# Top-32 attention with a token MLP on one core: the last batch in groups of three, three and two tiles instead of a group of its own for the last rows

## The chip, the cores and the metric

The kernel runs on one core of one Trainium2 chip. The metric is the device time of one execution in microseconds (us), the median of several runs.

## The reference

Eight batches, eight heads, 576 rows, head size 64, all float32. Each row of scores keeps its 32 largest values, a softmax is taken over these, and the values are weighed with it. The heads are put side by side into rows of 512, and a channel MLP with a normalization and a residual follows.

```python
scores = scale * np.matmul(q, k.transpose(0, 1, 3, 2))       # (8, 8, 576, 576)
kth = np.partition(scores, -32, axis=-1)[..., -32:-31]
scores = np.where(scores >= kth, scores, -1000000000.0)
scores = scores - np.max(scores, axis=-1, keepdims=True)
attn = np.exp(scores)
attn = attn / (np.sum(attn, axis=-1, keepdims=True) + 1e-09)
x = np.matmul(attn, v)                                       # then (8, 576, 512)
mu, var = mean and variance of x over the last axis          # cut
xn = (x - mu) / np.sqrt(var + 1e-06) * g_ln
out = x + np.maximum(xn @ w_ch1, 0.0) @ w_ch2                # 512 -> 2048 -> 512
```

## The kernel before

576 rows are four tiles of 128 rows (0 to 3) and one of 64, the "last rows" (tile `J = 4`). The kernel takes two heads at a time, so a batch has four head pairs (`hp`). A **unit** is one query tile of one head pair: its scores (TensorE), the choice of 32 values (VectorE, eight at a time), the mask and the exponential (ScalarE), and the turning of the weights so that keys lie on partitions. A unit of last rows holds both heads in one tile, and so is half of an ordinary one for VectorE. A **group** is the units of one job of one head pair that share one product with the values. The program is a loop over the units with index n, one step to each; the scores of a unit are made two steps ahead, and what follows its selection one to four steps behind.

The jobs are listed so:

```python
    for b in range(B):
        parts = [[0, 1], [2, 3], [J]]
        if b:
            parts = [[0, 1], [2, 3]]
            if b == B - 1:
                parts = [[J]] + parts
            else:
                parts[b < 2].append(J)
        for qts in parts:
            jobs += [Job(b, hp, [qts]) for hp in range(NHP)]
```

So batches 2 to 6 run the groups 0, 1, J for the four head pairs and then 2, 3 for the four; batch 7 runs J alone for four head pairs, then 0, 1, then 2, 3. There are 160 units, 20 to a batch.

From batch 2 on all units of a group but its last are turned by VectorE and DMA, not by TensorE (`moved`); a unit of last rows is never moved:

```python
    for u in units[jobs[5 * NHP].first :]:
        u.moved = not u.rest and u is not u.group.units[-1]
    ...
    def move(u):                       # moved: two VectorE transposes, then DMA out and back
        for t in range(2):
            nc.vector.transpose(blocks..., u.e[:, t, t * R : t * R + JP]...)
        nc.sync.dma_start(hbm[:], blocks)
        ...
    def turn(u):                       # not moved: four TensorE transposes to each head
        ...
                nc.tensor.transpose(ps[...], u.e[...], ident[:])
```

The product with the values is 9 matmuls whose width is the number of rows of the group, `g.nq`: 256, 320 or 64.

```python
    def values(g):
        for c in range(J):
            for h in range(2):
                nc.tensor.matmul(av[h * D : (h + 1) * D, 0 : g.nq], vb[:, h * J + c, :], ...)
        nc.tensor.matmul(av[:, 0 : g.nq], g.job.ends[:], g.pt[:, 2 * J, 0 : g.nq], ...)
```

When the last head pair of a group is through, its finished rows become a **block** of one, two or three tiles for the MLP. The last rows of two batches, 64 and 64, make one tile ("r"), which joins the block of the odd batch's group with J in it. The block's matmuls go into a list, `todo`, and are laid between the steps of the attention as filling work:

```python
    # block of n tiles, N = n * 128 rows; 4 chunks of 512 features, NF = 16 chunks of 2048
    hidden:  NF * NC = 64 matmuls, each N columns wide        # planned cost max(1.71e-3 * N, 0.31)
    project: n * NF matmuls, each 512 columns wide            # planned cost 1.71e-3 * 512
    turn:    n times 4 transposes                             # planned cost 0.44
    ...
            step = j.last + (3 if j.last < EARLY else 4)      # the step at which the block is given
            if J in j.groups[0].qts and b % 2:
                step += 1
                tiles.append(("r", b // 2))
    ...
    def slot(n):                       # filling work for each of the 8 slots of step n
        left = sum(t[1] for t in todo)
        if n > last_give:
            even = left / max(1, END - 1 - n)
        else:
            even = 99.0
            for m in sorted(gives):
                if m > n:
                    even = min(even, (left - RESERVE) / (m - n))     # RESERVE = 4.0
                    left += sum(b.cost() for b in gives[m])
        return max(0.0, even) / SLOTS
```

`slot` takes the smallest of the mean rates up to each later block, so that the filling work never runs out before a new block comes. The last block, tiles 2 and 3 of batch 7, is given at step 163; almost all of it runs after the attention is over. The list is worked off in order.

Of the kernel before, what the change touches and what calls it, by code (L numbers as in the profile page):

```python
# [21 lines left out]
J = 4  # L22
# [7 lines left out]
def kernel(  # L30
# [43 lines left out]
    B, H, S, D = q.shape  # L74
# [406 lines left out]
    def turn(u):  # L481

        g = u.group
        i0 = place_of(u)
        q0 = i0 * 32

        def part(t):
            ps = turned()
            for c in range(J):
                nc.tensor.transpose(  # L490
                    ps[:, c * P : (c + 1) * P], u.e[:, t, c * P + t * R : (c + 1) * P + t * R],
                    ident[:],
                )
            if u.rest:
                both = ps[:].rearrange("p (c h n) -> p h c n", h=2, n=R)
                for h in range(2):
                    nc.scalar.copy(
                        g.blocks[:, h, i0 : i0 + R // 32],
                        both[:, h].rearrange("p c (i n) -> p i c n", n=32),
                    )  # L500
            else:
                nc.scalar.copy(
                    g.blocks[:, t, i0 : i0 + P // 32],
                    ps[:].rearrange("p (c i n) -> p i c n", c=J, n=32),
                )

        def last():
            ps = turned()
            if u.rest:
                nc.tensor.transpose(ps[0:R, 0:P], u.e[:, 0, JP:S], ident[:])  # L510
                nc.tensor.transpose(ps[:, P : 2 * P], u.e[:, 0, JP - R : S], ident[:])
                for h in range(2):
                    nc.scalar.copy(  # L513
                        g.pt[h * R : (h + 1) * R, 2 * J, q0 : q0 + R],
                        ps[h * R : (h + 1) * R, h * (P + R) : h * (P + R) + R],
                    )
            else:
                ends = u.e[:].rearrange("p t n -> p (t n)")[:, JP : JP + P]
                nc.tensor.transpose(ps[:, 0:P], ends, ident[:])
                nc.scalar.copy(g.pt[:, 2 * J, q0 : q0 + P], ps[:, 0:P])  # L520

        heads = () if u.moved else range(len(u.tiles))
        return [lambda t=t: part(t) for t in heads] + [last]
# [206 lines left out]
    for b in range(B):  # L730
        parts = [[0, 1], [2, 3], [J]]
        if b:
            parts = [[0, 1], [2, 3]]
            if b == B - 1:
                parts = [[J]] + parts
            else:
                parts[b < 2].append(J)
        for qts in parts:
            jobs += [Job(b, hp, [qts]) for hp in range(NHP)]
    units = []  # L740
# [36 lines left out]
    for j in jobs:  # L777
        if j.hp == NHP - 1:
            b = j.b
# [114 lines left out]
    for n in range(END):  # L894
# [9 lines left out]
        parts = turn(ex) if ex else []  # L904
# [142 lines left out]
```

## Time and profile before

| | before |
|---|---|
| median of 3 runs | 1666.45 us |
| lowest, highest | 1665.65, 1667.94 us |
| span of the profiled execution | 1666.6 us |
| instructions profiled | 24932 |
| mean granted TensorE clock | 0.978 |

A float32 matmul of this kernel shows as two MATMUL records (a transpose as one). The ends of matmul records are modelled, so the time from the start of one record to the start of the next says more than its length. The first MAX8 of line L391 of a unit on VectorE is taken as the start of that unit's step, and all steps below are counted by it: unit 76 is the first of the last four units of batch 3, units 120 to 139 are batch 6, units 140 to 159 are batch 7.

### The profile page before, as it was taken

To read this page: it belongs to the slowest core of one execution; us is meant where nothing else is said; L and a number is where in the kernel's file an instruction comes from. 1 tells how busy PE (TensorE), PEld (TensorE's weight loads), DVE (VectorE), ACT (ScalarE), POOL (GpSimd) and SP (SyncE) were. 2 spreads that over 40 slices of the span, in tenths; PEclk is the share of its full clock that TensorE was granted. 3 is DMA by queue.
4 is the path that set the end of the run, shared out by engine and by line. 5 is a ranking of instruction groups with operands and counts; after the bars stand their busy time and mean duration, and the time that the engine had idled before them with its cause. 6 is when DMAs were issued, how large, how long until landed. Compare 5 with 4: busy or idle time off the path is not lost.

```text
span 1666.6 us, 24932 instructions
## 1 busy us (share of the span) xinstructions
PE 1566.9 (94%) x7057; PEld 941.7 (57%) x7057; DVE 1469.6 (88%) x4611; ACT 1042.4 (63%) x2615; POOL 671.5 (40%) x881
## 2 busy tenths in 40 slices
PE   2668989989899999999999999999999999999998
PEld 1336457556355474745547575745547575756764
DVE  5997999999999999999999999999879895988600
ACT  6886877667556665666656665656555565666620
POOL 5776763343442433343243433443243423333110
PEclk9879999999999999999999999999999999999999
DMA  7423332001442335333443335324333251222200
GB/s 176 106 72 95 85 64 58 21 14 22 100 110 84 99 85 132 93 88 89 108 123 92 86 104 126 97 71 99 99 97 97 72 115 46 61 78 70 80 13 13
DMA packets 303185, 139.30 MB, mean 84 GB/s; under 512 B 250820, under 2 KB 285640, under 8 KB 303048
## 3 DMA queue, kind: packets, MB, share of 16 engines
q1 hardware_dynamic: 298312, 137.12, 31.2%
q10 hardware_dynamic: 4736, 0.59, 0.3%
q8 instruction: 57, 0.93, 0.2%
q14 instruction: 80, 0.66, 0.1%
HBM read 92.54 MB, written 45.09 MB: 83 GB/s over the span
## 4 chain that ended last, share of the span: by engine, by line
PE 65%; DVE 23%; ACT 4%; issue 4%; POOL 3%; DMA 1%; SPq 0%; ACTq 0%; POOLq 0%; DVEq 0%
PE hps L664 23%; PE ops L680 22%; PE scps L354 7%; DVE m L399 7%; PE av L544 6%; DVE hi L386 6%; DVE hi L391 3%; DVE lo L386 2%; PE tp L490 2%; PE av L551 2%; DVE hi L375 2%; DVE size L193 1%; ACT sc L335 1%; POOL lo L376 1%; ACT e L426 1%
## 5 line engine op out<-in xcount | busy, mean ns | idle before, releaser
L664 PE MATMUL hps<-xT,w 128*128 128x256 f32 (+2 forms) x2176 | 553.3, 398 | 6.0 <-ACT xT L653 6.0
L680 PE MATMUL ops<-w,h 128*128 128x512 f32 x1152 | 548.0, 603 | 0.0
L399 DVE MAX8 m<-hi 128x8 f32<-128x304 f32 x1152 | 487.6, 458 | 3.3
L664 PEld LDWEIGHTS hps<-xT,w 128*128 128x128 f32 x2176 | 388.8, 192 | 111.4 <-issue 32.3
L376 POOL TENSOR_TENSOR lo<-sc,hi 128x576 int32<-128x576 int32 (+1 forms) x160 | 207.8, 1299 | 486.3 <-DVE hi L375 246.5
L386 DVE MATCH_REPLACE8 hi<-m,hi 128x304 f32<-128x304 f32 x864 | 389.4, 456 | 0.0
L680 PEld LDWEIGHTS ops<-w,h 128*128 128x128 f32 x1152 | 201.2, 192 | 187.2 <-issue 182.7
L391 DVE MAX8 hi<-lo 128x8 f32<-128x288 f32 x576 | 233.7, 441 | 39.3 <-POOL lo L379 38.2
L354 PE MATMUL scps<-kT,qT 64*128 64x288 f32 (+3 forms) x1344 | 220.7, 429 | 37.1 <-DVE qT L306 27.4
L335 ACT COPY sc<-scps 128x288 f32<-128x288 f32 x576 | 199.7, 408 | 68.2 <-PE scps L354 55.9
L426 ACT ACTIVATE e<-sc,m 128x576 f32<-128x576 f32 x288 | 224.1, 779 | 7.2 <-DVE m L399 4.0
L436 ACT ACTIVATE e<-e,bias 128x576 f32<-128x576 f32 x288 | 224.8, 781 | 0.7
L379 POOL TENSOR_TENSOR lo<-lo,sc 128x576 int32<-128x576 int32 (+1 forms) x160 | 206.9, 1293 | 12.5
L354 PEld LDWEIGHTS scps<-kT,qT 64*128 64x128 f32 (+1 forms) x1344 | 122.3, 179 | 152.9 <-issue 57.6
L544 PE MATMUL av<-pt,vb 128*64 128x256 f32 (+2 forms) x1152 | 148.8, 401 | 0.2 <-ACT pt L513 0.2
L675 ACT ACTIVATE h<-hps 128x512 f32<-128x512 f32 (+1 forms) x156 | 88.5, 567 | 86.1 <-PE hps L664 84.8
L375 DVE TENSOR_TENSOR hi<-sc 128x576 f32<-128x576 f32 (+1 forms) x160 | 115.0, 719 | 23.4 <-ACT sc L335 23.4
L556 ACT COPY oT<-av 128x256 f32<-128x256 f32 (+2 forms) x72 | 26.8, 372 | 160.3 <-PE av L551 160.3
L693 POOL TENSOR_TENSOR o<-o,x 128x512 f32<-128x512 f32 x32 | 42.0, 1313 | 209.6 <-ACT o L689 209.6
L386 DVE MATCH_REPLACE8 lo<-hi,lo 128x288 f32<-128x288 f32 x288 | 125.2, 441 | 0.0
L490 PE MATMUL tp<-ident,e 128*128 128x128 f32 x608 | 97.0, 284 | 25.3 <-ACT e L436 24.8
L544 PEld LDWEIGHTS av<-pt,vb 128*64 128x64 f32 x1152 | 76.0, 142 | 78.5 <-ACT sc L335 14.5
(70 smaller groups left out, 1259.5 us busy)
## 6 DMA issues: line engine op xcount, KB each, us to landing
turned<-sc SPq DMA_DIRECT2D x68, 512.0 KB, 2.6
pt<-turned SPq DMA_DIRECT2D x272, 128.0 KB, 3.0
vb<-in_v_dram SPq DMA_DIRECT2D x144, 128.0 KB, 2.6
raw<-in_moe_w_ch_dram SPq DMA_DIRECT2D x32, 512.0 KB, 4.0
kin<-in_k_dram SPq DMA_DIRECT2D x128, 72.0 KB, 2.5
qin<-in_q_dram SPq DMA_DIRECT2D x120, 72.0 KB, 2.5
out_dram<-o SPq DMA_DIRECT2D x32, 256.0 KB, 2.2
ends<-in_v_dram SPq DMA_DIRECT2D x144, 16.0 KB, 2.2
```

Of the source, the lines that this page charges most:

```text
L335: nc.scalar.copy(u.sc[:, t, s * HALF : (s + 1) * HALF], made[s][t][:, 0:HALF])
L354: nc.tensor.matmul(ps[i * R : i * R + ql, o : o + width], qT[r, q0 : q0 + ql], kT[r, k0 : k0 + width], start=True, stop=True,)
L376: nc.gpsimd.tensor_tensor(lo.bitcast(I32), a.bitcast(I32), hi.bitcast(I32), ALU.subtract)
L379: nc.gpsimd.tensor_tensor(lo.bitcast(I32), lo.bitcast(I32), b.bitcast(I32), ALU.add)
L386: nc.vector.match_replace(x[:, t], m[:, t, :], x[:, t], LOWEST)
L391: nc.vector.max(u.hi[:, t, o : o + 8], u.lo[:, t])
L399: nc.vector.max(m[:, t, :], u.hi[:, t])
L426: nc.scalar.activation(u.e[:, t], u.sc[:, t], AF.Prelu, bias=u.thr[:, t, 7:8], scale=-1.0, alpha=SLOPE)
L436: nc.scalar.activation(u.e[:, t], u.e[:, t], AF.Exp, bias=u.bias[:, t : t + 1], scale=-scale / SLOPE, accum_out=g.den[:, col : col + 1],)
L544: nc.tensor.matmul(av[h * D : (h + 1) * D, 0 : g.nq], vb[:, h * J + c, :], g.blocks[:, h, 0 : g.nq // 32, c, :], start=(c == 0), stop=False,)
L664: nc.tensor.matmul(ps["h"][:, o : o + N], w1[:, c, f * P : (f + 1) * P], xT[0][:, c, 0:N], start=(c == 0), stop=(c == NC - 1),)
L680: nc.tensor.matmul(ps[i][:], hT[f][:, i * P : (i + 1) * P], w2[:, f, :], start=(f == 0), stop=(f == NF - 1),)
```

## The change

Batch 7 loses its exception and is cut as batches 2 to 6 are: groups 0, 1, J for four head pairs, then 2, 3. The number of units stays 160, that of groups falls by four, and that of blocks by one: the tile of the last rows of batches 6 and 7 no longer is a block of its own early in batch 7, but the third tile of the block of tiles 0 and 1. The aim is that no group and no block has fewer than two tiles, so that no matmul of the MLP or of the values is narrower than 256 columns in these batches.

```diff
@@ -731,10 +731,7 @@
         parts = [[0, 1], [2, 3], [J]]
         if b:
             parts = [[0, 1], [2, 3]]
-            if b == B - 1:
-                parts = [[J]] + parts
-            else:
-                parts[b < 2].append(J)
+            parts[b < 2].append(J)
         for qts in parts:
             jobs += [Job(b, hp, [qts]) for hp in range(NHP)]
     units = []
```

## The prediction

> **What bounds the kernel now.** I read the page first, then the busy times by stage, then TensorE's own waits, then the pitch of single matmuls in the timeline.
>
> ```profile
> PE 1566.9 (94%) x7057; PEld 941.7 (57%) x7057; DVE 1469.6 (88%) x4611; ACT 1042.4 (63%) x2615; POOL 671.5 (40%) x881
> ...
> PE   2668989989899999999999999999999999999998
> ...
> DVE  5997999999999999999999999999879895988600
> ```
>
> TensorE is busy to the end; VectorE is nearly as busy up to about slice 29 and has holes after it. A busy TensorE need not be a full one, so I set two stages side by side: units 76 to 115 (from four units before batch 4 to the sixteenth of batch 5) and units 116 to 155 (the same places one double batch later), then the rest. Busy times of each engine in these three stretches:
>
> ```profile
> core 0: us, PE busy (x) PEld busy (x) DVE busy (x) ACT busy (x) POOL busy (x), PEclk, DMA share, GB/s
> 742.10:1114.20 372.10, 369.47 (x1631) 216.48 (x1630) 366.76 (x1152) 236.62 (x608) 145.09 (x203) 1.00 0.37 100
> 1114.20:1525.00 410.80, 407.47 (x1913) 246.87 (x1912) 363.13 (x1145) 245.40 (x629) 145.33 (x208) 1.00 0.31 83
> 1525.00:1666.60 141.60, 135.66 (x545) 87.59 (x543) 40.01 (x130) 46.48 (x107) 20.18 (x29) 0.99 0.12 36
> ```
>
> The first stretch has VectorE at 98.6% and TensorE at 99.3%, the second, 38.7 us longer, has VectorE at 88% and TensorE at 99%. So VectorE may be a second bound up to unit 115, but not after it. TensorE's own waits from unit 116 to the end (total us, times, longest):
>
> ```profile
> PE tp L648 <- ACT sc L335: 2.3, 3, 1.0
> PE hps L664 <- ACT xT L653: 1.1, 1, 1.1
> PE tp L490 <- ACT e L436: 0.4, 1, 0.4
> ```
>
> TensorE waits for some 4 us in the last 552. Is it full too? From the pitches below I gave every record the time its columns take (0.107 us a transpose, 0.215 us for 256 columns, half of that where two heads share the array) and summed: 343.0 us of work in the first stretch, 378.1 in the second, 131.5 in the third. Divided by the wall that is 0.922, 0.920 and 0.929. The three agree, and what is missing is spread over changes from one kind of matmul to another, not over waits. So **TensorE's work is the bound over all of the last 924 us**, and a change is worth what it takes from that work.
>
> The pitches, from the timeline of TensorE:
>
> ```profile
> 1018.77 2.37 PE L544 MATMUL av<-pt,vb 128*64 128x320 f32 x16
> 1021.07 0.81 PE L551 MATMUL av<-pt,ends 128*128 128x320 f32 x2
> 1021.72 1.02 PE L680 MATMUL ops<-w,h 128*128 128x512 f32 x2
> ...
> 1370.12 1.95 PE L544 MATMUL av<-pt,vb 128*64 128x256 f32 x16
> 1371.99 0.70 PE L551 MATMUL av<-pt,ends 128*128 128x256 f32 x2
> 1372.53 1.02 PE L680 MATMUL ops<-w,h 128*128 128x512 f32 x2
> ...
> 1400.94 0.69 PE L544 MATMUL av<-pt,vb 128*64 128x64 f32 x16
> 1401.55 0.43 PE L551 MATMUL av<-pt,ends 128*128 128x64 f32 x2
> 1401.82 0.60 PE L490 MATMUL tp<-ident,e 128*128 128x128 f32 x4
> 1402.27 0.27 PE L510 MATMUL tp<-ident,e 128*64 128x128 f32 x1
> ```
>
> From the start of a values product to the start of what follows it: 2.95 us at 320 columns, 2.41 at 256, 0.88 at 64. Four transposes take 0.45 us, 0.11 each. For the MLP's hidden layer (128 records to a block):
>
> ```profile
> 1498.61 2.17 PE L664 MATMUL hps<-xT,w 128*128 128x128 f32 x18
> 1500.62 0.27 PE L519 MATMUL tp<-ident,e 128*128 128x128 f32 x1
> ...
> 1605.94 27.89 PE L664 MATMUL hps<-xT,w 128*128 128x256 f32 x128
> 1633.67 27.63 PE L680 MATMUL ops<-w,h 128*128 128x512 f32 x64
> ```
>
> 18 records of the one-tile block in 2.01 us, 0.112 each; 128 of the two-tile block in 27.73 us, 0.217 each; 64 records of the projection in about 27.5, 0.43 each. The median pitch at 384 columns is 0.323.
>
> **What the Trainium skill says.** "Perfetto Trace Analysis", section Identifying the Most-Contended Engine, warns that matmul busy time does not tell how near TensorE is to its limit. The trace agrees: the 256-wide hidden records have a mean length of 385 ns at a pitch of 217, hence the sum of columns above. The same page, section Optimizing Tensor Performance, Matmuls, says that larger matmuls are more efficient where possible. That is the reason for the change; but "TensorE: Matmul & The Clock Gate", section Back-to-back issue gap, has the spacing grow with the columns, with a floor only at small widths (about 60 cycles up to 64 columns). Here 128 columns cost 0.112 us and 256 cost 0.217, a ratio of 1.94, so the one-tile block wasted little. Only the 64-wide values product shows a floor: a fifth of the columns at 0.30 of the time of 320.
>
> **The change part by part.**
>
> Values: four times 0.88 + 2.41 becomes four times 2.95. Saved 4 x 0.34 = 1.4 us of TensorE.
>
> Hidden layer: 128 x 0.112 + 128 x 0.217 = 42.1 us becomes 128 x 0.323 = 41.3. Saved 0.7 us. Projections and turns of the rows are the same in number.
>
> Turning: tile 1 of batch 7 is no longer the last of its group, so four more units are moved. Each drops 8 transposes: 32 x 0.11 = 3.5 us of TensorE, and the changes of kind around eight runs of transposes, which I put at 8 x 0.15 = 1.2 us (an estimate from the missing 8% of the stretches above). ScalarE loses 8 copies of 0.58 us, off the path.
>
> VectorE gains two transposes to each of the four units. The mean of one is 685 ns (89.3 us over 136 of them, line L468): 8 x 0.685 = 5.5 us. The DMA out and back is what batches 2 to 6 have, with TensorE not waiting for it. Loads of values fall from twelve sets to eight in batch 7, off the path.
>
> Where the work lies: the larger thing that moves. By the planned costs a block of one tile is 34.3 us, of two 56.9, of three 85.4. Before, at step 116, the smallest mean rate is the one up to step 163: (85.4 + 3 x 56.9 + 34.3 + 56.9) / 47 = 7.4 us a step. After, nothing new comes between steps 143 and 156, so the smallest is the one up to 156: (85.4 + 3 x 56.9) / 40 = 6.4 us, the rate that units 76 to 115 have now. Up to step 156 the program therefore repeats that stretch, and the three-tile block is left for seven steps at 85.4 / 7 = 12.2 us each. Up to step 116 nothing should change.
>
> That gives a second way to the time. Unit 156 starts at 1114.2 + 372.1 = 1486.3 us instead of 1525.0, 38.7 us earlier; the first stretch has five projection records fewer than the new one will have, 2.1 us, so 1488.4. What filling work is then left: before, 13 projection records and two blocks of two, 5.6 + 2 x 55.9 = 117.4 us. After, 16 records left over as at step 116 (6.9), the block of three (41.3 + 41.3 + 1.3 = 83.9) and the block of two (55.9), 146.7 us. The difference of 29.3 us, at 0.945 (the third stretch without the last 4 us, in which TensorE has ended), is 31 us. The end: 1488.4 + 141.6 + 31 = 1661.
>
> The first way: 1.4 + 0.7 + 3.5 + 1.2 = 6.8 us of work less, 1666.45 - 6.8 = 1659.6. The two agree within 1.5 us. **I predict 1660 us**, 0.4% faster.
>
> **The rivals.**
>
> VectorE becomes the bound (it has 5.5 us more, and 98.6% in the stretch that is repeated): its added time then lies on the path up to unit 155 and the work pushed to the end is not made up for: 1666 to 1670. For it speaks VectorE's share in the first stretch; against it, that TensorE's share of columns is 0.92 there too, so little TensorE time was lost.
>
> The crowded end: with 12.2 us of filling in a step of which VectorE needs 9 to 10, scores come late, units 156 to 159 take about 15 us each, and the last block starts late. If TensorE waits in the chain values, statistics, centring, of the last tiles, some 5 us are lost: 1665. Against it: six projections are kept for that chain, and 18 records (7.7 us) cover it today.
>
> Batch 7 was poor before: it takes 203.6 us from unit 140 to the end of its selection, batch 5 takes 186.7, and units 142 and 144 of the trace need 14.4 and 17.5 us. If those were lost time and not filling work, some 17 us come back: 1649. Against it: batch 6, cut as the others, takes 208.9 us at the same higher rate of filling, and TensorE has no wait above 1.1 us there.
>
> **Range and chances.** The savings are some 7 us if TensorE stays full; losing the chain at the end or to VectorE costs up to 6, and a better mesh gives up to 5. The range is 1655 to 1666. A change of 2% is 33 us, far outside any of these: 0.01 faster, 0.98 within, 0.01 slower.
>
> **What would show it.** Right: the same times up to unit 116; batch 6 at about 186 us instead of 208.9; unit 156 near 1488; then 15 us a unit with VectorE waiting; 576 transposes on L490 instead of 608, and 144 on L468 instead of 136; no 128-wide hidden records, and 64-wide values products in batch 0 alone; TensorE busy at 94% or a little more. Wrong: unit 156 later than 1493 (VectorE is the bound), TensorE waits of several us after unit 156, or work per column other than 0.92 of the wall.

## The result and the profile after

| | before | after |
|---|---|---|
| median | 1666.05 us (1664.49 to 1667.94, 4 runs) | 1659.92 us (1658.31 to 1660.92, 4 runs) |
| ratio, 95% interval | | 0.9962 (0.9945 to 0.9979) |
| span of the profiled execution | 1666.6 us | 1655.8 us |
| instructions profiled | 24932 | 24475 |

The change brings 6.1 us, 0.4%. First the page of the changed kernel, busy times and slices:

```profile
PE 1559.2 (94%) x6825; PEld 918.0 (55%) x6825; DVE 1472.6 (89%) x4619; ACT 1036.8 (63%) x2607; POOL 673.9 (41%) x879
...
PE   2668989989899999999999999999999999999998
...
DVE  5997999999999999999999999999999999997000
```

TensorE is as full as it was. VectorE no longer has holes: it is at 9 up to slice 36 and then stops, where before it had 5 to 8 in seven of the ten slices from 29 to 38. The same three stretches as in the prediction (units 76 to 115, 116 to 155, the rest), and batch 6 as a fourth; the columns are those of the table shown there:

```profile
739.70:1111.40 371.70, 369.63 (x1632) 216.59 (x1631) 366.34 (x1151) 236.51 (x609) 145.33 (x203) 1.00 0.37 100
1111.40:1484.70 373.30, 371.57 (x1641) 217.37 (x1640) 367.28 (x1151) 237.31 (x611) 144.93 (x203) 1.00 0.36 99
1484.70:1655.80 171.10, 165.47 (x584) 94.64 (x582) 40.96 (x132) 50.07 (x116) 22.41 (x32) 1.00 0.10 32
1150.50:1337.90 187.40, 186.77 (x802) 104.90 (x801) 183.04 (x574) 117.52 (x301) 72.47 (x102) 1.00 0.37 100
```

The second stretch now is a copy of the first, in time (373.3 and 371.7 us), in number of matmuls and in VectorE's work; before it took 410.8. The rest takes 171.1 instead of 141.6. What was gained by unit 155 was mostly paid after it, and the difference is the result: from unit 116 to the end 552.4 us became 544.4. The profiled execution was already 2.4 us ahead of that of before at unit 76, where nothing has changed; so from here on the stretch from unit 116 to the end stands beside the medians.

TensorE's waits from unit 116 to the end (total us, times, longest):

```profile
PE hps L664 <- ACT xT L653: 1.3, 2, 1.1
PE xo L583 <- ACT oT L556: 0.9, 2, 0.5
```

2.2 us instead of 4.1: the waits of L648, the turn of a block's rows, are gone. The groups that changed (count, then busy us and mean ns):

```profile
L664 PE MATMUL hps<-xT,w 128*128 128x256 f32 x1536 | 370.3, 386 | 3.0 <-ACT xT L653 3.0
...
L664 PE MATMUL hps<-xT,w 128*128 128x384 f32 x512 | 180.8, 493 | 3.2 <-ACT xT L653 3.2
...
L468 DVE STREAM_TRANSPOSE sc<-e 128x512 f32<-128x512 f32 x144 | 95.0, 697 | 21.4 <-ACT e L436 21.1
L490 PE MATMUL tp<-ident,e 128*128 128x128 f32 x576 | 92.0, 284 | 24.7 <-ACT e L436 24.2 <-ACT sc L335 0.5
...
L544 PE MATMUL av<-pt,vb 128*64 128x320 f32 x448 | 66.5, 439 | 0.0
...
L544 PE MATMUL av<-pt,vb 128*64 128x64 f32 x64 | 2.7, 228 | 0.2 <-ACT pt L513 0.2
```

There are 576 transposes on L490 and 144 on L468, no hidden record of 128 columns, and the 64-wide values products of batch 0 alone.

### The profile page after: what moved, and what is told of

It reads as the page before. It is cut to its first block, busy times and chain, and to the rows that moved or that the text cites. A ratio compares the mean times of both kernels' runs of the same rounds, so it can differ in the third digit from the quotient of the medians.

```text
span 1655.8 us, 24475 instructions
## 1 busy us (share of the span) xinstructions
PE 1559.2 (94%) x6825; PEld 918.0 (55%) x6825; DVE 1472.6 (89%) x4619; ACT 1036.8 (63%) x2607; POOL 673.9 (41%) x879
## 4 chain that ended last, share of the span: by engine, by line
PE 71%; DVE 18%; issue 4%; ACT 4%; POOL 3%; DMA 1%; ACTq 0%; POOLq 0%; DVEq 0%
PE hps L664 25%; PE ops L680 24%; PE scps L354 8%; PE av L544 7%; DVE m L399 5%; DVE hi L386 4%; DVE hi L391 3%; PE tp L490 2%; PE av L551 2%; DVE lo L386 2%; DVE hi L375 1%; DVE size L193 1%; PE tp L648 1%; ACT sc L335 1%; PE xo L583 1%
## 5 line engine op out<-in xcount | busy, mean ns | idle before, releaser
L664 PE MATMUL hps<-xT,w 128*128 128x256 f32 (+1 forms) x2048 | 551.1, 412 | 6.1 <-ACT xT L653 6.1
L680 PE MATMUL ops<-w,h 128*128 128x512 f32 x1152 | 548.7, 603 | 0.0
L399 DVE MAX8 m<-hi 128x8 f32<-128x304 f32 x1152 | 499.4, 479 | 3.3
L664 PEld LDWEIGHTS hps<-xT,w 128*128 128x128 f32 x2048 | 373.0, 192 | 122.7 <-issue 32.1
L386 DVE MATCH_REPLACE8 hi<-m,hi 128x304 f32<-128x304 f32 x864 | 398.4, 477 | 0.0
L680 PEld LDWEIGHTS ops<-w,h 128*128 128x128 f32 x1152 | 200.9, 192 | 186.4 <-issue 181.4
L391 DVE MAX8 hi<-lo 128x8 f32<-128x288 f32 x576 | 238.8, 458 | 12.7 <-POOL lo L379 11.6
L544 PE MATMUL av<-pt,vb 128*64 128x256 f32 (+2 forms) x1088 | 147.2, 413 | 0.2 <-ACT pt L513 0.2
L375 DVE TENSOR_TENSOR hi<-sc 128x576 f32<-128x576 f32 (+1 forms) x160 | 119.3, 746 | 21.3 <-ACT sc L335 21.3
L544 PEld LDWEIGHTS av<-pt,vb 128*64 128x64 f32 x1088 | 73.7, 142 | 77.7 <-ACT sc L335 15.9
L490 PE MATMUL tp<-ident,e 128*128 128x128 f32 x576 | 92.0, 284 | 24.7 <-ACT e L436 24.2
```

What stands on the lines that cost most here:

```text
L386: nc.vector.match_replace(x[:, t], m[:, t, :], x[:, t], LOWEST)
L391: nc.vector.max(u.hi[:, t, o : o + 8], u.lo[:, t])
L399: nc.vector.max(m[:, t, :], u.hi[:, t])
L664: nc.tensor.matmul(ps["h"][:, o : o + N], w1[:, c, f * P : (f + 1) * P], xT[0][:, c, 0:N], start=(c == 0), stop=(c == NC - 1),)
L680: nc.tensor.matmul(ps[i][:], hT[f][:, i * P : (i + 1) * P], w2[:, f, :], start=(f == 0), stop=(f == NF - 1),)
```

## The experiments

The theory: TensorE's work is the bound from unit 76 to the end, so the gain is the work taken from it (moving tile 1, wider products), and where the filling work lies does not matter. The rivals: VectorE is the bound up to unit 155; the gain is that of the pace (how much filling work a step gets); narrow matmuls cost much more than their columns; work pushed to the end lies bare.

The eight runs stand in two series with their own runs of before (medians 1666.68 and 1668.09 us), so ratios are to be compared. "Work" is the sum of columns from the prediction. The stretch from unit 116 on is that of the one profiled execution of each kernel; the two profiles of the changed kernel (after and same_chip_after) both give 544.4 us.

| run | median us | ratio to before, 95% | unit 116 to the end, us | of it work, us |
|---|---|---|---|---|
| before | | 1 | 552.4 | 509.7 |
| same_chip_after | 1659.57 | 0.9954 (0.9941 to 0.9968) | 544.4 | 506.2 |
| tile1_on_tensor | 1662.77 | 0.9973 (0.9963 to 0.9983) | 548.2 | 509.7 |
| rest_block_apart | 1659.57 | 0.9956 (0.9944 to 0.9969) | 544.6 | 506.2 |
| before_slow_pace | 1665.01 | 0.9985 (0.9977 to 0.9992) | 549.5 | 509.7 |
| before_tile1_moved | 1669.55 | 1.0009 (1.0001 to 1.0017) | 553.6 | 506.2 |
| before_slower_pace | 1688.12 | 1.0128 (1.0112 to 1.0143) | 573.8 | 509.7 |
| rest_in_last_group | 1659.60 | 0.9951 (0.9939 to 0.9964) | 543.0 | 506.2 |
| last_tiles_moved | 1656.78 | 0.9934 (0.9921 to 0.9946) | 541.9 | 503.7 |

**same_chip_after**: the changed kernel as it is.

> The changed kernel unaltered, as the measure for the others. Full TensorE: 1660 us, 0.996 of the kernel before. If the measured gain was chance: 1.000.

0.9954, as expected; the interval leaves out 1.

**tile1_on_tensor**: the changed kernel without the four more moved units.

```diff
         u.moved = not u.rest and u is not u.group.units[-1]
+        if u.job.b == B - 1 and u.qt == 1:
+            u.moved = False
```

> The changed kernel, but tile 1 of batch 7 is turned by TensorE again (32 transposes more there, 8 transposes of 0.685 us fewer on VectorE, 5.5 us). Theory (TensorE full all the way): 3.5 us of transposes and about 1 us of changes of kind come back, 1664.5 us. Rival (VectorE is the bound up to unit 155): its 5.5 us go, 1654.5 us.

It is 3.2 us slower than the changed kernel, 3.8 us from unit 116 on. The same two stretches from unit 116:

```profile
1114.00:1488.90 374.90, 373.16 (x1667) 219.49 (x1666) 361.97 (x1144) 240.32 (x615) 143.21 (x202) 1.00 0.32 87
1488.90:1662.20 173.30, 167.40 (x592) 95.67 (x589) 40.93 (x132) 51.70 (x120) 23.23 (x34) 1.00 0.10 31
```

VectorE is busy 5.3 us less in the first of them (361.97 for 367.28), and yet the stretch is 1.6 us longer. So VectorE's added transposes are not on the path, and TensorE's are: the rival falls. The 3.8 us are the 3.5 of the transposes and 0.3 more, which lie after TensorE's last matmul.

**rest_block_apart**: the changed kernel with the tile of last rows as a block of its own.

```diff
             if J in j.groups[0].qts and b % 2:
+                if b == B - 1:
+                    add_block(step, tiles, dsts)
+                    tiles, dsts = [], []
                 step += 1
                 tiles.append(("r", b // 2))
```

> The changed kernel, but the block of three is given as a block of two at step 155 and one of the last rows alone at step 156. Theory: 0.7 us more for the narrow hidden matmuls and 0 to 3 us of waiting for the turn of its rows, 1660.5 to 1663 us. Rival (narrow matmuls cost what the plan in the code counts for them, 34.3 + 56.9 - 85.4 = 5.8 us): 1666 us.

Nothing: 0.9956 and 0.9954, 0.2 us from unit 116 on. That is below the 0.7 us of the pitches, which the medians could not show anyway (the runs of this kernel lie between 1658.5 and 1662.0 us), and far from the 5.8 us that the plan in the code counts for it. Making the block wider was worth nothing that can be measured.

**before_slow_pace**: the kernel before with the pace of the changed one.

```diff
                     left += sum(b.cost() for b in gives[m])
+            if 116 <= n < 156:
+                even = min(even, 6.4)
```

> The kernel before with one line more: between steps 116 and 155 the filling work is held to 6.4 us a step, which is what the changed kernel has there, so some 39 us of it are pushed behind unit 155. Theory: TensorE stays full at either pace, so the time is that of before, 1666 us within 2, with unit 156 near 1486. Rival 1 (the gain comes from the pace): 1660 us. Rival 2 (pushed work is lost work): 1672 us or more.

```profile
1111.90:1489.70 377.80, 375.66 (x1743) 222.82 (x1742) 362.91 (x1146) 242.29 (x623) 145.86 (x206) 1.00 0.34 89
1489.70:1661.50 171.80, 166.50 (x715) 109.65 (x713) 40.27 (x130) 50.88 (x113) 22.22 (x31) 1.00 0.10 32
```

One line of pace moves unit 156 from 410.8 us after unit 116 to 377.8 after it, 33 us, and the time by 1.7 us. So filling work can be pushed 33 us back at no loss, as the theory says. But it is not nothing, as I had it: the interval, 0.9977 to 0.9992, leaves out 1, and from unit 116 on it is 2.9 us, a quarter to a third of all that the change brings. TensorE's waits say where 2 us of it come from:

```profile
PE hps L664 <- ACT xT L653: 1.1, 1, 1.1
PE xo L583 <- ACT oT L556: 1.0, 2, 0.5
```

The waits of L648 for ScalarE (2.3 us in the kernel before) are gone here too, with the order of before. They belong to the faster pace, not to the block of one tile.

**before_slower_pace**: the same with 5.4 instead of 6.4.

```diff
+            if 116 <= n < 156:
+                even = min(even, 5.4)
```

> As the slow pace, but 5.4 us of filling work a step between steps 116 and 155, another 39 us pushed behind. Theory: VectorE, at 363 of 378 us there with the pace of 6.4, is the bound below it: the stretch stays above 366 us and TensorE loses some 25 to 30 us in it, 1690 us. Rival (TensorE is the bound at any pace): 1665 us, with the stretch at about 338 us.

```profile
1111.80:1481.70 369.90, 348.16 (x1642) 203.53 (x1641) 360.65 (x1145) 237.37 (x627) 142.41 (x206) 0.99 0.34 91
1481.70:1685.50 203.80, 198.56 (x817) 130.25 (x815) 40.30 (x130) 50.37 (x110) 22.60 (x31) 1.00 0.09 28
```

```profile
PE tp L490 <- ACT e L436: 12.3, 6, 3.8
PE av L544 <- DMA pt<-turned: 5.8, 2, 2.9
PE scps L354 <- DVE qT L306: 2.4, 1, 2.4
PE hps L664 <- ACT xT L653: 1.1, 1, 1.1
```

Here the time is 20 us longer, and the stretch from unit 116 on 21 us. Units 116 to 155 shrink by only 8 us against the pace of 6.4 although 32 us of work left them: VectorE, 97.5% busy, does not allow less. TensorE's work is 315.4 us of 369.9, 0.85; at 0.92 it would have needed 343, so some 27 us are lost. The waits listed, 21.6 us, are nearly all for the attention's own chain. So the edge between the two bounds lies somewhere between 6.4 and 5.4 us a step; no pace between them was tried. Down to 6.4 pushing work back is free, and of what the pace of 5.4 pushes further most is lost (24 us of 32, by the stretch from unit 116 on).

**before_tile1_moved**: the moving alone, without the last rows behind it.

```diff
         u.moved = not u.rest and u is not u.group.units[-1]
+        if u.job.b == B - 1 and u.qt == 1:
+            u.moved = True
```

> The kernel before, with the turning of tile 1 of batch 7 given to VectorE and DMA, but without the last rows behind it in its group: the moving alone. Theory: the same 3.2 to 3.8 us as the moving brings in the changed kernel, 1663 us, if TensorE is so far behind that the DMA (about 8 us out and back in the trace of the changed kernel) has landed before the values product. Rival: the last rows at the end of the group are what hides it, and each of the four products waits some 4 us: 1663 + 16 = 1679 us.

Neither: 1.0009, 1.5 us slower, with 3.5 us less of work. The two moves that are waited for, in TensorE's timeline:

```profile
1491.36 1.60 PE L664 MATMUL hps<-xT,w 128*128 128x128 f32 x12
1494.17 1.95 PE L544 MATMUL av<-pt,vb 128*64 128x256 f32 x16 [1.21 <-DMA out_dram<-o]
1496.05 0.70 PE L551 MATMUL av<-pt,ends 128*128 128x256 f32 x2
...
1510.26 1.02 PE L680 MATMUL ops<-w,h 128*128 128x512 f32 x2
1513.34 2.98 PE L544 MATMUL av<-pt,vb 128*64 128x256 f32 x16 [2.05 <-DMA vb<-in_v_dram]
1516.25 1.22 PE L551 MATMUL av<-pt,ends 128*128 128x256 f32 x2
1517.26 1.15 PE L680 MATMUL ops<-w,h 128*128 128x512 f32 x2
```

By the stretch, 4.7 us are lost: 3.5 of work saved, and 1.2 longer. Two of the four products wait for a DMA, 3.3 us together. The transfers named are not the ones: they landed at 1494.35 and 1513.57 us, after the products had begun. The last piece of the turned weights landed at 1494.04, 0.13 us before the first of the two. The other two products had 0.7 and 0.4 us to spare; in the changed kernel the four products of tile 1 come 4.6 to 8.2 us after the last piece, with a unit of last rows (7.0 to 7.5 us) in between.

The remaining 1.4 us follow the longer wait. The product behind it takes 2.91 us to the start of L551, for 1.88 behind the other wait, and L551 1.01 for 0.53. The granted clock of these 3.5 us, and of the 4 us before them, is the number before the last two:

```profile
1514.00:1517.50 3.50, 3.50 (x15) 2.19 (x12) 3.50 (x11) 0.00 (x0) 0.39 (x2) 0.52 0.33 132
1510.00:1514.00 4.00, 1.95 (x12) 1.03 (x13) 4.00 (x16) 1.62 (x5) 2.81 (x2) 1.00 0.81 197
```

So part of what the change brings is this: the last rows at the end of the group give the DMA of tile 1 its time, and the moving, a loss of 1.5 us in the old order, is a gain of 3.2 in the new.

**rest_in_last_group**: the last rows behind tiles 2 and 3, so that the block of three is the last.

```diff
-            parts[b < 2].append(J)
+            parts[b < 2 or b == B - 1].append(J)
...
-    END = N + 6
+    END = N + 7
```

> The changed kernel, but the last rows of batch 7 go behind tiles 2 and 3 instead of 0 and 1 (and the loop is one step longer), so the last block has three tiles and the one before it two. TensorE's work is the same. Theory: the time is that of the changed kernel, 1660 us, plus what TensorE waits for the last rows at the end, 0 to 6 us. Rival (a long last block is time that nothing hides): its 28 us more lie bare, 1688 us.

```profile
1113.50:1494.60 381.10, 380.03 (x1695) 224.42 (x1694) 371.59 (x1175) 241.13 (x620) 144.98 (x202) 1.00 0.34 94
1494.60:1656.50 161.90, 155.87 (x532) 88.38 (x530) 35.45 (x108) 44.13 (x107) 21.17 (x33) 0.99 0.13 40
```

0.9951 beside 0.9954. The last block is 28 us longer, and the time does not notice: the turn of its rows starts at 1565.6 us instead of 1594.7 in same_chip_after, because the work that the last block now has no longer stands before it, and TensorE is full on either side.

**last_tiles_moved**: the changed kernel, with tile 3 of three head pairs moved as well.

```diff
         u.moved = not u.rest and u is not u.group.units[-1]
+        if u.i in (155, 157, 159):
+            u.moved = True
```

> The changed kernel, with units 155, 157 and 159 (tile 3 of three head pairs of batch 7) turned by VectorE and DMA as well, where VectorE has time to spare. Theory: 24 transposes at 0.11 us less on TensorE, 1657 us, if TensorE, which is behind there, does not wait for the DMA. Rival: the DMA of some 8 us is waited for, at the end at least, and the time is 1660 to 1668 us.

```profile
1485.00:1653.60 168.60, 162.82 (x560) 92.52 (x558) 44.90 (x138) 46.66 (x110) 22.43 (x32) 0.99 0.16 51
```

0.9934 beside 0.9954: about 3 us faster than the changed kernel, 11 us faster than before, and the best of all. From unit 116 on 24 transposes less are 2.5 us. These units are the last of their groups, as in before_tile1_moved, but TensorE does not wait: after unit 155 it has 12 us of filling work a step, and its values products come late enough after the move. VectorE's second transposes of the last unit (159) and the DMA that follows them, then the product that needs them:

```profile
1563.67 0.71 DVE L468 STREAM_TRANSPOSE sc<-e 128x512 f32<-128x512 f32 x1 [4.28 <-ACT e L436]
1564.41 0.34 SPq L473 DMA_DIRECT2D turned<-sc  x1
...
1567.06 1.73 SPq L476 DMA_DIRECT2D pt<-turned  x4
```

```profile
1569.74 6.17 PE L680 MATMUL ops<-w,h 128*128 128x512 f32 x14
1575.85 1.95 PE L544 MATMUL av<-pt,vb 128*64 128x256 f32 x16
```

The last piece landed at 1571.41, 7.0 us after the first issue and 4.4 us before the product; for units 155 and 157 the room is 7.0 and 5.6 us. Late filling work, which by itself gains little, pays for a DMA that is not hidden elsewhere.

## Why the prediction was right, and where its terms were off

**The bound.** Right. Work over wall from unit 116 on was 0.923 before and is 0.930 after. Taking VectorE's added 5.5 us away again made the kernel slower (tile1_on_tensor).

**The shape.** Right: unit 156 was to start 746.3 us after unit 76 and starts 745.0 after it; batch 6 was to take 186 us and takes 187.4; the rest was to take 172.6 and takes 171.1. The units after 155 were to take about 15 us each. Units 156 and 157 take 10.7 and 10.0 and only unit 158 14.6. Scores are made two steps ahead, which would put the effect of the higher pace two units late; that was not tried by itself. The sum is not touched by it. The sums of columns were made at 0.213 us for 256 columns instead of the 0.215 written (which gives 345.5, 380.9 and 132.5 us), and the 0.945 should be 0.956 (131.5 over 137.6); neither moves the forecast by as much as 1 us.

**The sum.** The 6.8 us had the right size, but not for all of the reasons given. By the stretch from unit 116 on, before to slow pace, slow pace to tile1_on_tensor, tile1_on_tensor to after:

| term | predicted us | measured us |
|---|---|---|
| pace alone | 0 | 2.9 (1.7 by the medians) |
| groups and blocks merged | 1.4 + 0.7 | 1.3 (2.2 by the medians) |
| tile 1 moved | 3.5 + 1.2 | 3.8 (3.2 by the medians) |
| sum | 6.8 | 8.0 (7.1 by the medians) |

Three terms were mis-sized. "The changes of kind around eight runs of transposes", put at 1.2 us, are nothing: beyond the 3.5 us of the transposes only 0.3 came, after TensorE's last matmul. In the trace of the changed kernel a hidden record of 256 columns is followed after 0.216 us by a transpose as by another hidden record, and a transpose after 0.109 us by either. The 8% that TensorE misses lie elsewhere (last section), so a mean over all was the wrong price for this one. The 0.7 us of the hidden layer are 0.2 or nothing. And the pace was taken as neutral; it brings 2 to 3 us, of which 2 are the waits of L648 that I had listed among TensorE's waits of before and had not counted as something the change could take away. That the sum came so near is in part luck: two terms were some 1.7 us too large together, and the one left out was 2 to 3 us.

The 1.4 us of the values have the right size, but not as "a floor" of narrow matmuls. In a 64-wide product the pairs of records follow each other after 0.058 us, about a quarter of the 0.216 at 256 columns. What made it dear is a fixed 0.36 us, which the products of 256 and 320 columns have as well (0.35 and 0.34); four products fewer save it four times.

**The rivals.** VectorE as the bound: fallen for this pace, right below it (before_slower_pace). The crowded end: did not come; the chain of the last tiles in the changed kernel is covered by more work than before, 26 records of L680 between the last product's L583 and the turn (L648), for 18:

```profile
1578.20 1.95 PE L544 MATMUL av<-pt,vb 128*64 128x256 f32 x16
...
1582.55 11.32 PE L680 MATMUL ops<-w,h 128*128 128x512 f32 x26
1593.71 1.04 PE L648 MATMUL tp<-ident,x 128*128 128x128 f32 x8
1594.59 1.02 PE L680 MATMUL ops<-w,h 128*128 128x512 f32 x2
1595.48 27.89 PE L664 MATMUL hps<-xT,w 128*128 128x256 f32 x128
```

Batch 7 as lost time: its slow units of before were filling work, as supposed; before_slow_pace takes 33 us out of units 116 to 155 and spends 30 of them later.

## What to carry to other kernels

Where one in-order engine is full from early on, a change of order is worth the work it takes from that engine and the waits it removes; sum its columns over long stretches and compare the quotient with the wall before pricing anything by the wall of a stage, for a stage that becomes 38 us shorter may give 30 of them back. How filling work is spread is nearly free as long as the other engine still has time to spare, and below that point most of it is lost. And a transfer that must be hidden before a product wants either other units behind it in its group or a place where the bounding engine is well behind.

## What the runs showed of the hardware

A matmul a quarter or a third as wide was hardly dearer per column (0.112 us a record at 128 columns, 0.217 at 256, 0.323 at 384, 0.43 at 512), and going to transposes and back cost nothing (0.216 and 0.109 us, as above). What cost was each group of half-array matmuls, where two heads share the array: the scores of a unit, and the L544 part of a values product. In the changed kernel:

```profile
1134.04 1.46 PE L664 MATMUL hps<-xT,w 128*128 128x384 f32 x4
1135.43 1.24 PE L354 MATMUL scps<-kT,qT 64*128 64x288 f32 x8
1136.60 2.20 PE L664 MATMUL hps<-xT,w 128*128 128x384 f32 x6
1138.73 1.95 PE L544 MATMUL av<-pt,vb 128*64 128x256 f32 x16
```

The four hidden records before the scores take 1.39 us, for 4 x 0.323 = 1.29. The four pairs of scores take 1.17, for four times the 0.242 from pair to pair in their middle, 0.97. The first hidden record after them takes 0.43 for 0.323. That is 0.40 us more for one group of scores; a group of last rows has 0.35 more, a values product 0.34 to 0.36. In units 116 to 155 of the changed kernel 40 groups of scores and 16 products come to 21.2 us, most of the 24.5 by which the 373.3 us exceed the sum of the steady spacings, 348.8.

Behind the wait of 2.05 us in before_tile1_moved the granted clock was at half for 3.4 us, and so it was twice in before_slower_pace, at waits of 2.9 and 2.4 us. Other waits of 2.3 to 3.8 us there left it at 1.00, so no length of wait can be named from these runs.
